# The second expert layer under a manual schedule, with whole 256-token units from the start and raw buffers given out by a planner

## The chip, the cores and the metric

The kernel runs on one core of one Trainium2 chip. The time is that of one execution on the device, in microseconds (us), from one launch; several executions are made and their median is given. Engines are named as in the profile: PE (matmul) and PEld (its weight loads), DVE, ACT, POOL, and SP, which only issues transfers here.

## What is computed

Three stages follow each other. The change touches the third.

```python
x = _attn_ref(q, k, v)                       # windowed attention with block sums, 2 x 8 x 768 x 64
x = x.transpose(0, 2, 1, 3).reshape(1536, 512)
x = _moe_ref(x, **moe)                       # each token through the one expert that its gate picks
# _moe2_ref: N = 1536 tokens, D = 512, E = 8 experts, F = 1024
logits = x @ w_gate
P = np.exp(logits - logits.max())
for _ in range(8):                           # rows, then columns, eight rounds
    P /= P.sum(1, keepdims=True) + 1e-09
    P /= P.sum(0, keepdims=True) + 1e-09
    P *= N / E
for e in range(E):                           # every token through every expert
    h = np.maximum(x @ w1[e], 0.0)
    out += P[:, e:e + 1] * (h @ w2[e])
```

## The kernel before

**Products.** Both products of an expert are done with seven block products in place of eight (sums and differences of operand blocks, Strassen's way), each operand as a high and a low f16 part, so three matmuls for each block. Tokens are taken in two halves of 768, each cut into three chunks of 256 columns. A unit is one chunk of one expert: its first products are 4 pieces (`fc`) of 7 block products of 6 matmuls, 168 matmuls in all, and its second products are 2 times 7 block products of 12 matmuls, again 168. `first(u, fc, i)` (line 1227 holds its matmul) and `second(e, k, s, i)` (line 1314) emit one block product each, and the ACT or DVE instruction that takes its result out of PSUM.

**Units before.** The first chunk of expert 0 is cut into two units of 128 columns, so that the first can begin when one block of 128 tokens is there: 25 units, `LEAD` = 1 more than 24.

**Ticks.** A list of ticks orders the emission: 28 a unit, one first product a tick. Other work is put on ticks by `at(tick, f)` and is emitted ahead of the product of that tick. Second products follow by a credit, in the long run one for two ticks. A product's block sums (lines 1247 to 1284) come 8 to 18 ticks after its piece began.

**PSUM.** The block products of a piece share two tiles (`x`, and `a` with its halves y and z), and results are taken out between the products that go into the same place: three ticks, or at the least two, lie between.

**Who decides the order.** An engine runs its instructions in the order of its own queue, and waits at the one whose inputs aren't there. Before, the whole block is emitted in ticks, and Tile's scheduler then sets each engine's order out of its own estimate of when each instruction is ready; the emission is only its priority. Around the blocks, one `issue_after` pins an instruction behind another.

**Weights.** For each expert 8 pieces (`Piece`) are brought in by SP (`load`, lines 677 to 683) into one of three buffers, `raws`, squared by ACT for a scale (`measure`, line 691; `rate`, line 697), negated by ACT (`signs`, line 707) and summed by accumulating transfers that POOL issues from SBUF to SBUF (`add`, line 702; `chain(1)` to `chain(3)`, each upon the result of the one ahead). ACT then writes the high parts (`hi`, line 724, as `raw_hi` and `sum_hi`) and DVE the low parts (`lo`, line 729). Offsets of these steps in ticks, and which of the three buffers a piece uses, are written out by hand (`lay`). The scaled result of a second product is written to one of two `y` tiles by ACT (line 1352) and added to `acc` by an accumulating transfer of POOL's (lines 1346, 1354).

**Tokens and routing.** `tokens(j)` brings one pair of 128-token blocks (`load`), turns them by PE (`turn`, line 1057, ACT copy 1064), makes the seven operands (`operands`: DVE 1077 to 1086, ACT casts 1069, low parts 1070 on POOL or DVE) and the `logits`. `mixing()` is the routing: 5 steps to start, 8 rounds of two, an end.

Of the kernel before, what the change touches and what calls it, by code (L numbers as in the profile page):

```python
# [108 lines left out]
def body(ctx: ExitStack, tc: tile.TileContext, q, k, v, wg1, w1a, w2a, wg2, w1b, w2b, cst, out):  # L109
# [928 lines left out]
    def tokens(j):  # L1038
# [3 lines left out]
        xw, ps, tmp = [], [], []  # L1042
# [10 lines left out]
        def turn():  # L1053
            for half in range(2):
                p = pg.tile([P, KC, P], F32, tag="x", name="pt")
                for kc in range(KC):
                    nc.tensor.transpose(p[:, kc], xw[half][:, kc * P : (kc + 1) * P], ident)
                t = half * HTB + j
                nc.gpsimd.tensor_copy(xinv[:, t : t + 1], xw[half][:, DM : DM + 1])
                if half == 0:  # L1060
                    tmp.append(raws[2].rearrange("p a f -> p (a f)"))
                to = tmp[0] if half == 0 else xw[0]
                to = to[:, :DM].rearrange("p (k t) -> p k t", k=KC)
                nc.scalar.copy(to, p)
                ps.append(to)
# [6 lines left out]
        def operands():  # L1072
            t4 = tmp[0][:, DM:].rearrange("p (k t) -> p k t", k=2 * KC)
# [125 lines left out]
    def spot(u, b):  # L1199

        seq = u - LEAD - CHUNKS + 1
        if seq < 0:
            return sets[UNITS[u][1]], b
        return (xh, xl), (7 * seq + b) % 8
# [7 lines left out]
    def first(u, fc, i):  # L1212

        e, k, o, n = UNITS[u]
# [9 lines left out]
        p = s["x"][:, :n] if place == "x" else s["a"][:, "zy".index(place), :n]  # L1224
        for kc in range(K2):
            for m, (l, r) in enumerate(((wh, sh), (wh, sl), (wl, sh))):
                nc.tensor.matmul(  # L1227
                    p, l[:, a, kc * P : (kc + 1) * P], r[:, j, kc, o : o + n], start=new and kc == 0 and m == 0,
                    stop=kc == K2 - 1 and m == 2, skip_group_check=True,
                )  # L1230
        c, k_ = s["c"][:, :, :n], kap[e % 2][:, fc : fc + 1]
# [13 lines left out]
        elif i == 4:  # L1245
            add(slice(C1, C0 + 1), s["a"][:, :, :n])
# [8 lines left out]
    def operands2(u, fc):  # L1255

        e, k, o, n = UNITS[u]
        c = st.pop((u, fc))["c"][:, :, :n]
# [3 lines left out]
        def raw_hi():  # L1262
            if o == 0:
                old = CHUNKS * e + k - 2
                while old >= 0 and rest and rest[0][:2] <= divmod(old, CHUNKS):
                    second(*rest.pop(0))
                hs[e, k, fc] = tuple(hg.tile([P, 7, CN], F16, tag=x, name="h" + x) for x in "hl")
            h.extend(x[:, :, o : o + n] for x in hs[e, k, fc])
# [104 lines left out]
    ra, rb, rc = raws  # L1373
    spare = [acc[:, t : t + 2].rearrange("p a (b d) -> p (a b) d", d=Q) for t in (4, 10)]
    for e in range(1, E):
        s = TICKS * (LEAD + CHUNKS * e)
        p1, p2, level = weights(e)

        def lay(p, raw, load, measure=True, begin=None):
            at(s + load, lambda: p.load(raw))  # L1380
            if measure:
                junk = raw[:, 4:6].rearrange("p a f -> p (a f)") if raw in raws else acc[:, 3]
                at(s + load + 5, lambda: p.measure(junk.bitcast(BF16)))
                at(s + load + 8, p.rate)
            if begin is None:
                return
            at(s + load + 6, p.signs)
            mid = load + 11
            if p.second:
                at(s + mid, lambda: p.chain(1))  # L1390
                mid += 4
            at(s + mid, lambda: p.chain(2))
            if p.second and p.j == F2 - 1:
                last[e] = p
                return
            begin = max(begin, load + 9)
            at(s + begin, p.raw_hi)
            at(s + begin + 1, p.raw_lo)
            end = max(mid + 4, begin + 3)
            at(s + end, lambda: p.chain(3))  # L1400
            at(s + end + 4, p.sum_hi)
            at(s + end + 5, p.sum_lo)

        if e == 1:
            lay(p2[0], rb, -45, begin=-30)
            lay(p2[1], ra, -40, begin=-30)
            lay(p1[0], rc, -32, begin=-15)
            lay(p2[3], spare[0], -22)
            lay(p1[3], spare[1], -22)
            lay(p1[1], rb, -19, begin=-8)  # L1410
            lay(p2[2], spare[0], -14)
            lay(p1[2], ra, -13, begin=-1)
            lay(p1[3], rc, -4, False, begin=6)
            lay(p2[2], rb, 2, False, begin=0)
            lay(p2[3], ra, 10, False, begin=0)
        else:
            lay(p2[3], rc, -66)
            lay(p2[0], rb, -58, begin=-45)
            lay(p2[1], rc, -52, begin=-45)
            lay(p2[2], ra, -45, begin=0 - 45)  # L1420
            lay(p1[0], rb, -32, begin=-15)
            lay(p1[3], rc, -26)
            lay(p1[1], rc, -19, begin=-8)
            lay(p1[2], ra, -13, begin=-1)
            lay(p1[3], rb, -4, False, begin=6)
            lay(p2[3], ra, 10, False, begin=0)
        at(s - 3, level)
        for k in range(CHUNKS):
            u = LEAD + CHUNKS * e + k
            b0 = TICKS * (u - 1)  # L1430
            for j, b in enumerate(ORDER):
                at(b0 + 5 if j == 0 else b0 + 7 * (F2 - 1) + FIRST[j - 1][0] + 1, lambda u=u, b=b: refill(u, b))

# [9 lines left out]
    COST2 = 3 * F2 * 109  # L1443
    LAG = 6 * 218 * 6
    ended = {}
    now = credit = 0
    for tick in range(max(ticks) + 8):
        for f in plan.pop(tick, ()):
            f()
        if tick in ticks:  # L1450
            u, fc, i = ticks[tick]
            e, k, o, n = UNITS[u]
            first(u, fc, i)
            cost = 6 * (109 if n == CN else 56)
            now += cost
            credit = min(credit + cost, COST2)
            if (fc, i) == (F2 - 1, 6):
                ended[e, k, o // P] = now
                if n == CN:
                    ended[e, k, 1] = now  # L1460
        if rest and (credit >= COST2 or rest[0][:2] == (0, 0)):
            e, k, s, i = rest[0]
            if now >= ended.get((e, k, s), now) + LAG:
                second(*rest.pop(0))
                credit -= COST2
                now += COST2
    for x in rest:
        second(*x)
    rest.clear()
# [24 lines left out]
```

## Time and profile before

| | us |
|---|---|
| median of 2 runs (lowest, highest) | 1427.23 (1426.74, 1427.72) |
| the profiled execution's own time | 1419.92 |
| its span, first to last instruction | 1418.1 |
| PE busy / PEld busy | 1237.8 / 1073.8 |
| DVE / ACT / POOL busy | 924.4 / 893.0 / 389.0 |
| mean granted clock of TensorE | 0.953 |

The busy times overlap. A matmul's record is longer than its place in the pipeline, so a PE that is busy in every row is not yet at its full pace. An idle row is put down to the engine that released it; idle time costs something only on the engine that sets the end.

### The profile page before, as it was taken

What the parts mean: (1) busy time and instruction counts of PE and PEld (TensorE: products, weight loads), DVE (VectorE), ACT (ScalarE), POOL (GpSimd) and SP (SyncE); (2) the same over time, 40 slices, a digit from 0 to 9 for tenths busy, and PEclk for the clock granted to TensorE, in tenths of its full rate; (3) what the DMA queues carried; (4) which work ended last, traced back from release to release, by engine and by line L of the source; (5) the groups of instructions that cost most, each with busy time, mean ns of one, the idle gap of its engine ahead of it and who ended that gap; (6) DMA issues with size and microseconds to landing.
All of it is one profiled execution on the core that took longest, in us unless ns stands there. A gap on an engine that the chain in (4) does not pass through costs nothing.

```text
span 1418.1 us, 28331 instructions
## 1 busy us (share of the span) xinstructions
PE 1237.8 (87%) x10719; PEld 1073.8 (76%) x10719; DVE 924.4 (65%) x1825; ACT 893.0 (63%) x1691; POOL 389.0 (27%) x450
## 2 busy tenths in 40 slices
PE   6898877898889897889888897988798889789998
PEld 5776776788777786778777776877686778678887
DVE  6775655565878876666666656667566656666665
ACT  5685656665768677666766666666667666656541
POOL 4443222312322222331423232233312331321000
PEclk8999998899999999999999999999999999999999
DMA  9946886764545656575766576566747565753311
GB/s 208 198 99 212 259 235 197 210 189 151 169 149 121 130 142 154 111 159 122 162 149 137 107 152 153 120 143 131 162 104 168 118 135 125 156 120 88 82 47 53
DMA packets 213040, 206.67 MB, mean 146 GB/s; under 512 B 36816, under 2 KB 184144, under 8 KB 212512
## 3 DMA queue, kind: packets, MB, share of 16 engines
q1 hardware_dynamic: 162464, 143.22, 34.9%
q0 software_dynamic: 50432, 61.56, 26.2%
q8 instruction: 86, 1.41, 0.4%
q14 instruction: 58, 0.48, 0.1%
HBM read 135.57 MB, written 15.53 MB: 107 GB/s over the span
## 4 chain that ended last, share of the span: by engine, by line
PE 28%; DMA 19%; issue 11%; DVE 8%; ACT 6%; POOL 2%; SPq 1%; POOLq 0%; ACTq 0%; DVEq 0%
DMA raw<-raw 12%; PE gx L1314 8%; PE fx L1227 8%; PE ga L1314 6%; PE fa L1227 5%; DMA raw<-in_moe_w 5%; DVE w1l L729 3%; POOL raw L702 2%; ACT w1h L724 2%; ACT raw L691 1%; ACT w2h L724 1%; DVE w2l L729 1%; DMA xh<-xohd 1%; ACT c L1234 1%; DMA xl<-xold 1%
## 5 line engine op out<-in xcount | busy, mean ns | idle before, releaser
L1227 PEld LDWEIGHTS <-w1h 128*128 128x128 f16 x2800 | 270.3, 99 | 149.7 <-issue 113.6
L702 POOL DMA_DIRECT2D raw<-raw x256 | 226.0, 978 | 539.7 <-DMA raw<-raw 206.1
L1314 PEld LDWEIGHTS <-hh 128*128 128x128 f16 x2688 | 269.1, 100 | 45.7 <-issue 9.0
L1227 PE MATMUL fx<-xh,w1h 128*128 128x256 f16 (+1 forms) x768 | 207.5, 273 | 91.8 <-ACT c L1234 90.4
L1314 PE MATMUL gx<-w2h,hh 128*128 128x256 f16 x768 | 213.4, 278 | 4.0 <-ACT y L1352 2.3
L1314 PE MATMUL gx<-w2l,hh 128*128 128x256 f16 x768 | 213.4, 278 | 0.0
L1314 PE MATMUL gx<-w2h,hl 128*128 128x256 f16 x768 | 213.1, 278 | 0.0
L1227 PE MATMUL fx<-xh,w1l 128*128 128x256 f16 (+1 forms) x768 | 208.3, 274 | 0.0
L1227 PE MATMUL fx<-xl,w1h 128*128 128x256 f16 (+1 forms) x768 | 208.1, 273 | 0.0
L1234 ACT ACTIVATE c<-fx,kap 128x256 f32<-128x256 f32 (+1 forms) x300 | 136.4, 460 | 55.5 <-PE fx L1227 52.3
L1227 PE MATMUL fa<-xh,w1h 128*128 128x256 f16 (+1 forms) x576 | 155.2, 272 | 12.1 <-ACT c L1234 9.2
L1314 PE MATMUL ga<-w2h,hh 128*128 128x256 f16 x576 | 161.6, 281 | 2.9 <-ACT acc L1338 2.6
L1284 DVE TENSOR_TENSOR hl<-c,hh 128x1024 f16<-128x1024 f32 (+1 forms) x100 | 118.1, 1181 | 70.3 <-ACT hh L1281 69.6
L1314 PE MATMUL ga<-w2l,hh 128*128 128x256 f16 x576 | 161.4, 280 | 0.0
L1314 PE MATMUL ga<-w2h,hl 128*128 128x256 f16 x576 | 161.2, 280 | 0.0
L1227 PE MATMUL fa<-xh,w1l 128*128 128x256 f16 (+1 forms) x576 | 154.7, 271 | 0.9 <-DVE w1l L729 0.9
L1227 PE MATMUL fa<-xl,w1h 128*128 128x256 f16 (+1 forms) x576 | 155.0, 271 | 0.0
L1227 PEld LDWEIGHTS <-w1l 128*128 128x128 f16 x1400 | 138.8, 99 | 18.2 <-DVE w1l L729 1.2
L1314 PEld LDWEIGHTS <-hl 128*128 128x128 f16 x1344 | 134.5, 100 | 18.4
L1281 ACT CAST hh<-c 128x1024 f16<-128x1024 f32 (+1 forms) x100 | 101.0, 1010 | 58.2 <-DVE c L1278 57.7
L1272 DVE SCALAR_TENSOR_TENSOR hl<-c,hh 128x768 f16<-128x768 f32 (+1 forms) x100 | 94.1, 941 | 55.2 <-ACT hh L1269 55.2
L724 ACT ACTIVATE w1h<-raw,wsc 128x768 f16<-128x768 f32 (+1 forms) x64 | 66.7, 1042 | 92.8 <-DMA raw<-raw 66.3
(249 smaller groups left out, 2550.7 us busy)
## 6 DMA issues: line engine op xcount, KB each, us to landing
raw<-in_moe_w SPq DMA_DIRECT2D x64, 512.0 KB, 4.3
raw<-raw POOLq DMA_DIRECT2D x256, 128.0 KB, 3.7
raw<-in_moe_w SPq DMA_DIRECT2D x228, 128.0 KB, 3.3
xh<-xohd SPq DMA_DIRECT2D x147, 128.0 KB, 3.4
xl<-xold SPq DMA_DIRECT2D x147, 128.0 KB, 3.2
acc<-y POOLq DMA_DIRECT2D x72, 256.0 KB, 4.0
raw<-in_moe_w SPq DMA_DIRECT2D x38, 256.0 KB, 3.8
vt<-in_v SPq DMA_DIRECT2D x16, 240.0 KB, 8.1
```

What stands on the lines that cost most here:

```text
L691: nc.scalar.activation(junk, raw, AF.Square, accum_out=ssq_)
L702: nc.gpsimd.dma_start(out=self.raw[:, to], in_=self.raw[:, of], accum_op=ALU.add)
L724: nc.scalar.activation(self.dst()[0][:, w], self.raw[:, s], AF.Copy, scale=wsc[self.x][:, self.i : self.i + 1])
L729: nc.vector.scalar_tensor_tensor(out=lo[:, w], in0=self.raw[:, s], scalar=wsc[self.x][:, self.i : self.i + 1], in1=hi[:, w], op0=ALU.mult, ...
L1227: nc.tensor.matmul(p, l[:, a, kc * P : (kc + 1) * P], r[:, j, kc, o : o + n], start=new and kc == 0 and m == 0, stop=kc == K2 - 1 and m == ...
L1234: nc.scalar.activation(c[:, q], p, f, scale=k_)
L1272: nc.vector.scalar_tensor_tensor(out=h[1][:, :3], in0=raw, scalar=0.0, in1=h[0][:, :3], op0=ALU.max, op1=ALU.subtract)
L1281: nc.scalar.copy(h[0][:, 3:], c)
L1284: nc.vector.tensor_tensor(out=h[1][:, 3:], in0=c, in1=h[0][:, 3:], op=ALU.subtract)
L1314: nc.tensor.matmul(p, l, r, start=new and f == 0 and m == 0, stop=f == F2 - 1 and m == 2, skip_group_check=True)
```

## The change

The third stage is emitted under `tc.manual_schedule()`: each engine's order is the order of emission, and no scheduler moves it. Expert 0 has three units of 256 columns as the others have, so two pairs of token blocks are loaded, turned and made into operands ahead of the first product (70 small matmuls on ones stand between their loads and their turns), with scratch tiles of their own for the second pair. The other four pairs and the routing get new ticks. The three raw buffers are given out by a planner: each piece has a tick at which it is wanted, and gets the buffer that is free first; `load` is put at that tick or when the buffer is free, and the other steps at fixed distances (square 5, rate 8, signs 6, chains 11 and 15, high parts 4 ticks behind the last chain).

```diff
-        xw, ps, tmp = [], [], []
+        xw, ps = [], []
+        if j == 1:
+            tmp = yp.tile([P, DM], F32, tag="y", name="x1"), tp.tile([P, 4, CN], F32, tag="c", name="x4").rearrange("p a f -> p (a f)")
+        else:
+            t_ = raws[2].rearrange("p a f -> p (a f)")
+            tmp = t_[:, :DM], t_[:, DM:]
...
-                p = pg.tile([P, KC, P], F32, tag="x", name="pt")
+                p = (pf_ if j == 1 else pg).tile([P, KC, P], F32, tag="x", name="pt")
...
-    UNITS = [(0, 0, 0, P), (0, 0, P, P)] + [(0, k, 0, CN) for k in range(1, CHUNKS)]
-    UNITS += [(e, k, 0, CN) for e in range(1, E) for k in range(CHUNKS)]
-    LEAD = len(UNITS) - E * CHUNKS
+    UNITS = [(e, k) for e in range(E) for k in range(CHUNKS)]
...
     pairs = [tokens(j) for j in range(HTB)]
     mix = mixing()
+    pairs[0][0]()
+    pairs[1][0]()
     warm(pz, "m", 70)
-    for f in pairs[0][:3]:
-        f()
-    pairs[1][0]()
-    for j, ticks in enumerate(((0,), (2, 4, 20), (8, 28, 30, 46), (32, 40, 42, 48), (44, 57, 61, 64), (61, 64, 66, 72))):
+    for i in (1, 2):
+        pairs[0][i]()
+        pairs[1][i]()
+    for j, ticks in enumerate(((2,), (4,), (0, 3, 6, 20), (1, 12, 15, 24), (20, 33, 36, 48), (21, 42, 45, 52))):
         for tick, f in zip(ticks, pairs[j][-len(ticks) :]):
             at(tick, f)
-    for i, f in enumerate(mix):
-        at(74 + 2 * i, f)
+    turns = [76 + t + 5 * i for i in range(8) for t in (-3, 0)]
+    for tick, f in zip([52, 54, 58, 62, 66] + turns + [115], mix):
+        at(tick, f)
...
-            at(s + load, lambda: p.load(raw))
-            if measure:
...
-            lay(p2[3], rc, -66)
-            lay(p2[0], rb, -58, begin=-45)
-            lay(p2[1], rc, -52, begin=-45)
...
+            jobs += [(s - 70, p2[3], None, True), (s - 58, p2[0], s - 45, True), (s - 52, p2[1], s - 45, True), (s - 45, p2[2], s - 45, True)]
+            jobs += [(s - 32, p1[0], s - 15, True), (s - 26, p1[3], None, True), (s - 19, p1[1], s - 8, True), (s - 13, p1[2], s - 1, True)]
+            jobs += [(s - 4, p1[3], s + 6, False), (s + 10, p2[3], -99, False)]
...
+    free = [47] * len(raws)
+    for want, p, begin, measure in sorted(jobs, key=lambda x: x[0]):
+        i = min(range(len(raws)), key=lambda i: (max(free[i], want), -free[i]))
+        load = max(free[i], want)
+        s = TICKS * CHUNKS * p.e
+        at(load, lambda p=p, i=i: p.load(raws[i]))
+        if measure:
+            junk = raws[i][:, 4:6].rearrange("p a f -> p (a f)").bitcast(BF16)
+            at(load + 5, lambda p=p, junk=junk: p.measure(junk))
+            at(load + 8, p.rate)
...
+        if begin is not None:
+            at(load + 6, p.signs)
+            mid = load + 11
+            if p.second:
+                at(mid, lambda p=p: p.chain(1))
+                mid += 4
+            at(mid, lambda p=p: p.chain(2))
...
+                begin = max(begin, load + 9)
+                at(begin, p.raw_hi)
+                at(begin + 1, p.raw_lo)
+                end = max(mid + 4, begin + 3)
+                at(end, lambda p=p: p.chain(3))
+                end += 5
+                at(end - 1, p.sum_hi)
+                at(end, p.sum_lo)
...
-    for tick in range(max(ticks) + 8):
-        for f in plan.pop(tick, ()):
-            f()
...
+    with tc.manual_schedule():
+        for tick in range(max(ticks) + 8):
+            for f in plan.pop(tick, ()):
+                f()
```

In the kernel after, expert e begins with tick 84 e.

## Rows read from the trace of the kernel before

**Rows 1.** Windows: length, busy (count) of PE, PEld, DVE, ACT, POOL; clock, DMA share, GB/s.
```profile
359.50:467.58 108.08, 96.96 (x1107) 84.56 (x1105) 90.55 (x234) 85.39 (x185) 33.86 (x36) 0.98 0.54 147
467.58:609.08 141.50, 123.33 (x1065) 105.73 (x1063) 99.77 (x220) 95.14 (x165) 42.04 (x48) 0.95 0.61 134
609.08:1314.02 704.94, 620.44 (x5419) 538.75 (x5416) 448.30 (x812) 455.67 (x781) 198.81 (x228) 0.96 0.63 135
1314.02:1387.47 73.45, 73.14 (x670) 65.24 (x668) 49.74 (x87) 37.62 (x60) 2.61 (x3) 1.00 0.20 58
1387.47:1418.10 30.63, 26.08 (x235) 22.66 (x232) 14.03 (x26) 3.22 (x4) 0.00 (x0) 1.00 0.14 52
```

**Rows 2.** Window of line 1227 (first products) alone, PE and PEld.
```profile
609.08:1314.02 704.94, 347.75 (x2689) 264.92 (x2688) 0.96 0.63 135
```

**Rows 3.** Waits of PE from 609.08 to 1314.02: total us, times, longest.
```profile
PE fx L1227 <- ACT c L1234: 74.1, 35, 5.0
PE fa L1227 <- ACT c L1234: 8.3, 8, 2.3
PE gx L1314 <- ACT y L1352: 2.0, 3, 0.9
```

**Rows 4.** Waits of ACT from 609.08 to 1314.02.
```profile
ACT w1h L724 <- DMA raw<-raw: 52.4, 19, 4.6
ACT hh L1281 <- DVE c L1278: 36.8, 42, 1.9
...
ACT raw L691 <- DMA raw<-in_moe_w: 27.2, 20, 4.0
ACT c L1247 <- DVE c L1237: 25.8, 32, 1.3
ACT w2h L724 <- DMA raw<-raw: 25.5, 7, 5.6
```

**Rows 5.** Timeline of ACT: start, us, instruction, idle before it and releaser.
```profile
714.34 0.47 ACT L1234 ACTIVATE c<-fx,kap 128x256 f32<-128x256 f32 x1 [0.33 <-PE fx L1227]
717.09 1.15 ACT L724 ACTIVATE w1h<-raw,wsc 128x1024 f16<-128x1024 f32 x1 [2.27 <-DMA raw<-raw]
```

**Rows 6.** Timeline of POOL in the same microseconds.
```profile
713.76 0.86 POOL L702 DMA_DIRECT2D raw<-raw  x1 [1.72 <-DVE w1l L729]
```

**Rows 7.** The page's transfers: count, KB of one, median us from issue to landing.
```profile
raw<-raw POOLq DMA_DIRECT2D x256, 128.0 KB, 3.7
raw<-in_moe_w SPq DMA_DIRECT2D x228, 128.0 KB, 3.3
...
acc<-y POOLq DMA_DIRECT2D x72, 256.0 KB, 4.0
```

**Rows 8.** Groups by form from 609.08 to 1314.02: busy us, mean ns, idle before.
```profile
L702 POOL DMA_DIRECT2D raw<-raw x164 | 144.5, 978 | 310.6 <-DMA raw<-raw 120.8 <-ACT raw L707 99.0 <-DVE w1l L729 35.2
...
L1234 ACT ACTIVATE c<-fx,kap 128x256 f32<-128x256 f32 x193 | 89.1, 466 | 31.4 <-PE fx L1227 29.6 <-PE pf L697 1.7
...
L1352 ACT ACTIVATE y<-gx,pws 128x256 f32<-128x256 f32 x128 | 59.6, 466 | 18.8 <-PE gx L1314 18.8
```

**Rows 9.** Timeline of PE: the third stage's first matmul on a low part.
```profile
361.04 0.22 PE L1227 MATMUL fx<-xl,w1h 128*128 128x128 f16 x1
```

**Rows 10.** Groups from 353 to 420, ACT's and POOL's work on token blocks.
```profile
L1070 POOL TENSOR_TENSOR xl<-raw,xh 128x512 f16<-128x512 f32 x7 | 9.7, 1444 | 8.4 <-ACT xh L1069 8.3
L1069 ACT CAST xh<-raw 128x512 f16<-128x512 f32 (+1 forms) x16 | 8.6, 565 | 1.5 <-DVE raw L1081 1.5
...
L1064 ACT COPY raw<-pt 128x512 f32<-128x512 f32 x12 | 7.0, 593 | 11.3 <-PE pt L1057 11.3
```

**Rows 11.** Timeline of ACT, a result of a unit of 128 columns.
```profile
362.18 0.36 ACT L1234 ACTIVATE c<-fx,kap 128x128 f32<-128x128 f32 x1
```

**Rows 12.** Windows of 20 us: one with a long wait of PE's, one without.
```profile
1220.00:1240.00 20.00, 15.02 (x115) 12.14 (x113) 10.43 (x21) 11.84 (x21) 6.41 (x9) 0.83 0.78 153
1300.00:1320.00 20.00, 20.00 (x185) 17.93 (x184) 11.21 (x19) 12.05 (x21) 1.72 (x2) 1.00 0.45 117
```

More of the change, by code (lines that the diff above doesn't have):

```diff
@@ L1262, in raw_hi @@
         def raw_hi():
[L1263 to L1268, printed above, removed]
+            while u >= 2 and rest and rest[0][:2] <= UNITS[u - 2]:
+                second(*rest.pop(0))
+            h.extend(hg.tile([P, 7, CN], F16, tag=x, name="h" + x) for x in "hl")
+            hs[e, k, fc] = h
             nc.scalar.activation(h[0][:, :3], raw, AF.Relu)
@@ L1369, in body @@
             at(tick, f)
-    for i, f in enumerate(mix):
-        at(74 + 2 * i, f)
+    turns = [76 + t + 5 * i for i in range(8) for t in (-3, 0)]
+    for tick, f in zip([52, 54, 58, 62, 66] + turns + [115], mix):
+        at(tick, f)
     last = {}
-    ra, rb, rc = raws
     spare = [acc[:, t : t + 2].rearrange("p a (b d) -> p (a b) d", d=Q) for t in (4, 10)]
+    jobs = []
     for e in range(1, E):
-        s = TICKS * (LEAD + CHUNKS * e)
+        s = TICKS * CHUNKS * e
         p1, p2, level = weights(e)
-        def lay(p, raw, load, measure=True, begin=None):
-            at(s + load, lambda: p.load(raw))
-            if measure:
[L1382 to L1402, printed above, removed]
-        if e == 1:
[L1405 to L1415, printed above, removed]
-        else:
-            lay(p2[3], rc, -66)
-            lay(p2[0], rb, -58, begin=-45)
-            lay(p2[1], rc, -52, begin=-45)
[L1420 to L1427, printed above, removed]
@@ L1428, in body @@
+        at(s - 2, level)
         for k in range(CHUNKS):
[L1429 removed]
+            u = CHUNKS * e + k
             b0 = TICKS * (u - 1)
@@ L1432, in body @@
                 at(b0 + 5 if j == 0 else b0 + 7 * (F2 - 1) + FIRST[j - 1][0] + 1, lambda u=u, b=b: refill(u, b))
+    free = [47] * len(raws)
[8 more added lines that the diff above has]
+            at(load + 8, p.rate)
+            assert load + 8 <= s - 3, (p.e, p.second, p.j, load - s)
+            end = load + 5
+        if begin is not None:
[5 more added lines that the diff above has]
+            at(mid, lambda p=p: p.chain(2))
+            if p.second and p.j == F2 - 1:
+                last[p.e] = p
+                end = s + 39
+                assert mid < s + 30, (p.e, p.second, p.j, mid - s)
+            else:
+                begin = max(begin, load + 9)
[6 more added lines that the diff above has]
+                at(end, p.sum_lo)
+                assert end <= s + (39 if p.second else 7 * p.j + 1), (p.e, p.second, p.j, end - s)
+                assert begin <= s + (37 if p.second else 7 * p.j - 1), (p.e, p.second, p.j, begin - s)
+        free[i] = end + 1
     ticks = {}
@@ L1442, in body @@
             rest += [(e, k, s, i) for s in range(2) for i in range(7)]
-    COST2 = 3 * F2 * 109
-    LAG = 6 * 218 * 6
+    COST1, COST2 = 3 * K2 * 109, 3 * F2 * 109
+    LAG = 6 * (COST1 + COST2 // 2)
     ended = {}
     now = credit = 0
-    for tick in range(max(ticks) + 8):
-        for f in plan.pop(tick, ()):
-            f()
[L1450 to L1469, printed above, removed]
+    with tc.manual_schedule():
+        for tick in range(max(ticks) + 8):
+            for f in plan.pop(tick, ()):
+                f()
+            if tick in ticks:
+                u, fc, i = ticks[tick]
+                e, k = UNITS[u]
+                first(u, fc, i)
+                now += COST1
+                credit = min(credit + COST1, COST2)
+                if (fc, i) == (F2 - 1, 6):
+                    ended[e, k] = now
+            if rest and (credit >= COST2 or rest[0][:2] == (0, 0)):
+                e, k, s, i = rest[0]
+                if now >= ended.get((e, k), now) + LAG:
+                    second(*rest.pop(0))
+                    credit -= COST2
+                    now += COST2
+        for x in rest:
+            second(*x)
+        rest.clear()
     assert not plan, sorted(plan)
```

31 lines of the change are left out of this document (17 added, 14 removed).

## The prediction

> **What bounds the kernel now.** I read the windows by stretch first. The third stage goes from 359.5 to 1418.1 us, and its cuts fall on the first products of an expert or a unit: expert 0 takes 108.08 us, expert 1 141.50, the next 16 units 704.94, the last two units 73.45, the tail of second products 30.63 [rows 1]. The 16 units are known by their 2689 first products, 168 to the unit [rows 2]. The reader should see two things. The last two units, where no weights are prepared any more, run 670 PE records in 73.45 us at clock 1.00: 0.1096 us for one, 36.7 us a unit. The 16 units ahead of them take 44.1 each, though they do the same products. At 0.1096 us their 5419 records would take 594 us, so 111 us of the 704.94 are lost; expert 1's 1065 records would take 117, so 25 are lost.
>
> Next come the waits. In the 16 units PE waits 84.4 us, nearly all for an ACT instruction that should have cleared PSUM [rows 3]. The mean clock is 0.96 there; with two levels, full and half, that is half clock for 8% of the stretch, 56 us, of which half is lost: 28 us. The sum of 84.4 and 28 is 112, so the loss is accounted for. Then ACT's own waits: 105.1 us for transfers of weights, up to 5.6 us at a time (52.4, 25.5 and 27.2 us), and 62.6 for DVE, none over 1.9 us [rows 4]. ACT is busy 455.67 of 704.94 us and DVE 448.30 [rows 1], so neither is full. ACT stops at a weight piece, its queue holds the clearing of PSUM behind it, and PE runs dry.
>
> One case shows how. POOL issued the last accumulating transfer of a piece at 713.76 [rows 6]; ACT's writing of the sums' high part was next on its queue, waited 2.27 us and began at 717.09 [rows 5], that is 3.3 us after the issue. The emission puts the two four ticks apart; a tick at full pace is 36.7 / 28 = 1.31 us, so 5.2 us. The scheduler had moved them together: the order which ran is not that of the emission, and it counts on transfers quicker than the chip's 3.3 to 3.7 us [rows 7].
>
> **The parts, with their costs.** The sum is made against the profiled execution's own 1419.92 us; the median of the runs is 7.3 above it, and that is added at the end. Attention and the first expert layer aren't touched: 0.
>
> *The 16 units.* The manual order removes no instruction and adds none; it puts each at its tick. Squares stand 5 ticks behind their load (6.5 us; four issues and a landing of 3.3 [rows 7]), a chain's link 4 ticks or more behind the one ahead and the high part 4 behind the last link: 5.2 us against 3.7 to landing [rows 7], which leaves 1.5 us for POOL's own queue, where one issue takes 0.98 [rows 8]. Two issues ahead of it would use that up, so a rest of waits stays. On the other side, a product of the same PSUM place comes two or three ticks later, some 2.6 us, and an ACT result takes 0.47 [rows 8], so a wait of about 2 us on ACT is free. The order between loads, refills and the other buffers' loads on SP stays that of ticks, and SP has little to do. Bounds: 111 us gained if nothing is left; nothing gained if ACT's waits only change places. I take 85%, since what goes is the waits over 2 us and what stays is the rest of 1 us or less: -94. The clock's 28 us go with the waits in this, since it stood at 1.00 in a stretch of unbroken products and at 0.83 around a wait of 5 us [rows 12].
>
> Here the Trainium skill gives another measure. Rows first: PE's matmul records cover 620.44 of the 704.94 us, weight loads 538.75, or 76.4%, against 65.24 of 73.45, or 88.8%, at full pace [rows 1]. The page "Perfetto Trace Analysis", section "Identifying the Most-Contended Engine", says that matmul busy time judges headroom badly, as matmuls are pipelined, and that weight-load busy time is the better measure. By matmul records 84.5 us are open, by the page 704.94 x (1 - 76.4 / 88.8) = 98, by the count of products 111; at 85% that would be 72, 84 and 94. The trace bears the page out against the matmul records, and the count goes a step further.
>
> The skill also has a price for the chain's transfers. "DMA: Bandwidth & Descriptors", section "Anatomy of one DMA — SWDGE (gpsimd) path", fits 2.0 us plus the bytes over 436e3; for 128 KB that is 2.3 us, an estimate by that page. The row has 3.7. By the page the four ticks leave 2.9 us and no rest of waits, and the 16 units would give the whole 111; the sum goes by the row.
>
> *Expert 1.* The same mechanism with the end of the routing beside it: 25 us lost, at 85% -21, bounds 0 and -25. Its first pieces come at other ticks than later ones; ACT's 95.14 us and DVE's 99.77 in 141.50 [rows 1] still fit into 120.
>
> *The start.* Before, the first product came at 359.5 [rows 1] with half the columns, and its low-part matmuls only at 361.04 [rows 9], when POOL's difference was there. After, it needs the second pair as well. Behind the first pair ACT does two copies (0.59 each) and four more casts (0.57) ahead of that [rows 10], 3.4 us, then POOL's difference of 1.44 as before. DVE's sums lie between the casts: up to 2.5 more. PE then stands still for about 5 us between turning the tokens and its first product, and such a gap was followed by a clock of 0.83 over 20 us, 3.4 us lost [rows 12]. Together +3.4 to +9.3; I take +6.
>
> *Expert 0.* Two units of 128 columns become one of 256: the same columns for PE, 168 matmuls fewer, nothing gained there. For ACT a result of 128 columns takes 0.36 us [rows 11] and one of 256 takes 0.47 [rows 8], so a pair costs 0.25 more than one; at 16 such results in the unit, and some 12 longer instructions of each engine with the like saving, 5 to 7 us of ACT and as many of DVE go away. DVE is the fullest engine here, 90.55 of 108.08 us [rows 1], with tokens' and routing work on it. The tokens' transfers on SP wait for the raw buffers, as before; they can start ahead of their tick, as SP waits for nothing else. Moving this work earlier by ticks puts more on the first unit, where no second product stretches the ticks: ACT and DVE will bind it. Bounds: PE's idle 11.1 us gained, or, at the density that DVE reaches in expert 1 (99.77 of 141.50, 71%), 90.55 / 0.71 = 128, 20 lost. I take -5.
>
> *The planner.* It only moves some loads by a few ticks; each piece's steps keep their distances, and the weights' last part is still written ahead of its first use by 6 ticks or more. 0, with the two bounds inside those of the 16 units. *Last units and tail*: same work, 0.
>
> Sum: -94 - 21 + 6 - 5 = -114. 1419.92 - 114 = 1306, plus 7.3: **1313 us**.
>
> **Rivals.** (a) *ACT and DVE in lockstep.* With fixed orders ACT's 62.6 us of waits for DVE [rows 4] can't be filled with other work any more and pass to PE in full: 16 units take 594 + 63 = 657, a gain of 48, expert 1 gains 10, the start as above: 1419.92 - 57 + 7.3 = 1370. For it: ACT would be busy 455.67 of 594, 77%, and no stretch of before runs unbroken at that density. Against it: those waits are under 1.9 us each, and the PSUM distance covers 2.
>
> (b) *The change doesn't do what it says.* If the order that ran is in the main the emission's, only latencies count and nothing moves: 1427, between 1400 and 1450. For it: the distances in ticks are those of before. Against it: the case of 713.76 to 717.09 [rows 5, 6].
>
> (c) *Slower: POOL's queue in strict order.* A chain's link that waits for the one ahead now holds the accumulation of `y` into `acc` behind it; a `y` tile comes back late, ACT waits ahead of line 1352 and holds PE. There are 72 such transfers [rows 7]. If each came 2.5 us late, that is 180 us, and 1427 - 114 + 180 = 1493. It decides from 114 / 72 = 1.6 us each. For it: POOL waited 120.8 us for its own chains in 164 issues [rows 8]. Against it: PE waited only 2.0 us on `y` before [rows 3], and a tile has about 6 ticks, 7.9 us, against an issue and 4.0 to landing [rows 7].
>
> **How the numbers follow.** Forecast 0.70, (a) 0.13, (b) 0.10, (c) 0.07. The forecast's lower end: the 16 units and expert 1 lose nothing more (-136), expert 0 gains 11, the start costs 3: 1419.92 - 144 + 7 = 1283; and the fullest 20 us hold 185 records at 0.108 [rows 12], against 0.1096, which takes another 8 from the 16 units: 1275. The upper end takes in (a), 1370, with the 20 us that expert 0 could lose: 1390. So 1275 to 1390, which leaves out (b) and (c). A measurement of this kernel tells 2% from no change. Faster by over 2%, below 1399: the forecast, (a) and a little of (b), 0.83. Slower by over 2%: 0.07. Between: 0.10.
>
> **What would show it.** Right: a unit of experts 2 to 6 near 38 us; PE's waits on line 1234 under 20 us in those units, ACT's waits for weight transfers under 25, clock 0.99, weight loads busy 86% or more. The first product of the stage around 364 to 367; expert 0 about 108 us from its first product. Wrong would be: ACT's waits for transfers as before (then the order wasn't the cause), or gone while PE still waits for line 1234, now behind DVE (a), or POOL's line 702 with ACT's line 1352 behind it (c), or an expert 0 of 120 us and more, with DVE full. What could upset the forecast most is the density of ACT and DVE, which no stretch of before shows at full pace.

## The result, and the profile after

The changed kernel takes 1362.89 us (median of 2 runs, 1360.79 and 1365.00) against 1427.23: 0.9549 of before, interval 0.9484 to 0.9614. The forecast was 1313, its range 1275 to 1390. The gain is 64 us where 114 were expected. The profiled execution's own time is 1360.79, so the sum to account for is 1419.92 - 1360.79 = 59.1.

The windows of the kernel after, cut as those of before [rows 1] (length, then busy and count of PE, PEld, DVE, ACT, POOL, then clock, DMA share, GB/s). Lines 1 to 3 are the units of expert 0, 4 to 6 those of expert 1, then the 16 units, the last two, the tail:

```profile
365.80:401.70 35.90, 28.35 (x281) 23.59 (x281) 25.64 (x46) 20.78 (x41) 8.88 (x12) 0.80 0.44 163
401.70:449.00 47.30, 41.83 (x392) 36.34 (x390) 32.49 (x65) 29.61 (x59) 8.98 (x10) 0.93 0.29 86
449.00:492.10 43.10, 34.05 (x280) 28.07 (x279) 33.26 (x94) 30.23 (x54) 10.58 (x13) 0.92 0.63 149
492.10:538.80 46.70, 42.55 (x375) 36.86 (x373) 40.12 (x94) 27.02 (x48) 12.25 (x15) 0.96 0.55 119
538.80:581.20 42.40, 38.93 (x343) 33.91 (x341) 31.58 (x62) 32.27 (x56) 11.20 (x13) 0.96 0.56 125
581.20:624.50 43.30, 38.39 (x342) 33.64 (x340) 28.86 (x60) 30.58 (x53) 15.27 (x18) 0.96 0.76 161
624.50:1246.10 621.60, 597.89 (x5418) 528.19 (x5417) 456.54 (x818) 450.60 (x787) 203.34 (x233) 1.00 0.71 155
1246.10:1319.40 73.30, 72.12 (x661) 64.49 (x660) 50.34 (x87) 35.91 (x60) 2.61 (x3) 1.00 0.22 62
1319.40:1359.00 39.60, 29.05 (x243) 24.35 (x240) 15.01 (x27) 3.31 (x4) 0.00 (x0) 0.91 0.11 41
```

Against [rows 1] the stage splits like this (us):

| | forecast | measured | before to after |
|---|---|---|---|
| start | +6 | +6.3 | first product at 359.5, 365.8 |
| expert 0 | -5 | +18.2 | 108.1, 126.3 |
| expert 1 | -21 | -9.1 | 141.5, 132.4 |
| 16 units | -94 | -83.3 | 704.9, 621.6 |
| last two units | 0 | -0.1 | 73.4, 73.3 |
| tail | 0 | +9.0 | 30.6, 39.6 |
| sum | -114 | -59.0 | |

So the 16 units did nearly what was forecast, and 44 of the missing 55 us lie outside of them. The waits of PE in the 16 units (total, times, longest), to set against 74.1 and 8.3 us in [rows 3]:

```profile
PE fx L1227 <- ACT c L1234: 13.1, 18, 1.4
PE pf L697 <- DVE sqb L692: 9.6, 11, 1.5
PE fa L1227 <- ACT c L1234: 0.3, 1, 0.3
```

The waits of ACT there, to set against [rows 4]:

```profile
ACT hh L1279 <- DVE c L1276: 28.8, 23, 3.7
ACT w1h L724 <- DMA raw<-raw: 27.5, 16, 3.7
...
ACT raw L691 <- DMA raw<-in_moe_w: 23.6, 16, 2.8
ACT w2h L724 <- DMA raw<-raw: 15.0, 5, 3.3
```

ACT still waits 27.5 + 23.6 + 15.0 = 66.1 us for transfers (105.1 before), but PE's wait for the clearing of PSUM is down from 82.4 to 13.4 and the clock is 1.00. By the page both kinds of transfers land later than before; the chain's was 3.7 and the load's 3.3 [rows 7]. A second profile of the same kernel has 3.9 for the chain, so this difference alone isn't the reason for ACT's waits; it is looked for below:

```profile
raw<-raw POOLq DMA_DIRECT2D x256, 128.0 KB, 4.5
raw<-in_moe_w SPq DMA_DIRECT2D x228, 128.0 KB, 3.8
```

By the Trainium skill's page "Perfetto Trace Analysis", section "Identifying the Most-Contended Engine", weight-load busy time is the better measure of what is open: 528.19 / 621.60 = 85.0% here against 64.49 / 73.30 = 88.0% in the last two units. By that, an estimate of 21 us is left in the 16 units; a later run found 25 (18.6 against the second profile), so the traces agree with the page.

In expert 0 PE's waits from 365.8 to 492.1 name few places:

```profile
PE fa L1227 <- ACT c L1234: 9.5, 2, 5.1
PE pf L697 <- DVE gsc L627: 4.9, 2, 2.7
PE fx L1227 <- ACT xh L1071: 3.4, 1, 3.4
```

ACT's timeline at the first of them (start, length, instruction, idle before it):

```profile
384.76 0.61 ACT L1071 CAST acc<-raw 128x512 f16<-128x512 f32 x1
388.62 1.49 ACT L1071 CAST acc<-raw 128x512 f16<-128x512 f32 x3 [3.26 <-DVE raw L1080]
390.01 0.40 ACT L1087 CAST bh<-raw 128x256 f16<-128x256 f32 x1
390.32 0.63 ACT L1247 ACTIVATE c<-c 128x512 f32<-128x512 f32 x1
390.85 0.45 ACT L1234 ACTIVATE c<-fa,kap 128x256 f32<-128x256 f32 x1
```

A token pair's casts (`acc` and `bh` in the lines) stand as one block on ACT's queue, because they are emitted on one tick. ACT stops 3.26 us inside the block until DVE has the operands ready, and the clearing of `fa`, for which PE waits, stands behind the block. The cause is that of before, with another owner: then a weight piece held the queue, now a token pair does.

The tail, on DVE's timeline and PE's:

```profile
1326.80 1.23 DVE L1282 TENSOR_TENSOR hl<-c,hh 128x1024 f16<-128x1024 f32 x1 [1.11 <-ACT hh L1279]
1327.94 0.48 DVE L1342 SCALAR_TENSOR_TENSOR acc<-ga,pws,acc 128x256 f32<-128x256 f32 x1
...
1328.47 0.37 PE L1312 MATMUL ga<-w2h,hh 128*128 128x256 f16 x1 [4.86 <-DVE acc L1342]
```

The closing ticks hold the sums of the last piece and no second product, as the credit grows with first products alone. So DVE's queue has all those sums ahead of the result that frees PE's place: 4.86 us of stand, and then half clock (mean 0.91 in the tail).

### The profile page after: what moved, and what is told of

Same layout as the page of the kernel before. It is cut to its first block, busy times and chain, and to the rows that moved or that the text cites. A ratio compares the mean times of both kernels' runs of the same rounds, so it can differ in the third digit from the quotient of the medians.

```text
span 1359.0 us, 27981 instructions
## 1 busy us (share of the span) xinstructions
PE 1220.4 (90%) x10551; PEld 1066.1 (78%) x10551; DVE 938.3 (69%) x1793; ACT 879.6 (65%) x1663; POOL 388.7 (29%) x450
## 4 chain that ended last, share of the span: by engine, by line
PE 23%; DMA 15%; issue 8%; ACT 7%; DVE 4%; SPq 1%; POOL 1%; ACTq 0%; POOLq 0%; DVEq 0%
DMA raw<-raw 9%; PE gx L1312 7%; PE fx L1227 6%; PE ga L1312 5%; DMA raw<-in_moe_w 5%; PE fa L1227 4%; ACT hh L1279 2%; ACT raw L691 2%; ACT c L1234 1%; DMA acc<-y 1%; POOL raw L702 1%; DVE acc L1342 1%; DVE w2l L729 1%; ACT raw L707 1%; DVE w1l L729 1%
## 5 line engine op out<-in xcount | busy, mean ns | idle before, releaser
L1312 PEld LDWEIGHTS <-hh 128*128 128x128 f16 x2688 | 264.8, 99 | 47.4 <-issue 15.2
L1227 PE MATMUL fx<-xh,w1h 128*128 128x256 f16 x736 | 202.7, 275 | 21.7 <-ACT c L1234 16.7
L1227 PE MATMUL fx<-xl,w1h 128*128 128x256 f16 x736 | 202.9, 276 | 1.4 <-POOL xl L1072 1.4
L1227 PE MATMUL fx<-xh,w1l 128*128 128x256 f16 x736 | 202.8, 276 | 0.0
L1234 ACT ACTIVATE c<-fx,kap 128x256 f32<-128x256 f32 x288 | 132.2, 470 | 58.0 <-PE fx L1227 52.6
L1227 PE MATMUL fa<-xh,w1h 128*128 128x256 f16 x552 | 152.5, 276 | 4.7 <-ACT c L1234 4.7
L1227 PE MATMUL fa<-xl,w1h 128*128 128x256 f16 x552 | 152.6, 276 | 0.0
L1227 PE MATMUL fa<-xh,w1l 128*128 128x256 f16 x552 | 152.4, 276 | 0.0
L1282 DVE TENSOR_TENSOR hl<-c,hh 128x1024 f16<-128x1024 f32 x96 | 117.3, 1222 | 49.0 <-ACT hh L1279 48.9
L1312 PEld LDWEIGHTS <-hl 128*128 128x128 f16 x1344 | 132.4, 99 | 16.2
L1279 ACT CAST hh<-c 128x1024 f16<-128x1024 f32 x96 | 99.8, 1040 | 43.7 <-DVE c L1276 43.3
L790 DVE TENSOR_TENSOR wl<-raw,wh 128x1024 fp32r<-128x1024 f32 x64 | 78.1, 1223 | 41.3 <-ACT wh L789 38.4
```

Source lines behind the costliest of these rows:

```text
L790: nc.vector.tensor_tensor(out=lo, in0=raw, in1=hi.bitcast(F32), op=ALU.subtract)
L1227: nc.tensor.matmul(p, l[:, a, kc * P : (kc + 1) * P], r[:, j, kc], start=new and kc == 0 and m == 0, stop=kc == K2 - 1 and m == 2, skip_gr ...
L1234: nc.scalar.activation(c[:, q], p, f, scale=k_)
L1279: nc.scalar.copy(h[0][:, 3:], c)
L1282: nc.vector.tensor_tensor(out=h[1][:, 3:], in0=c, in1=h[0][:, 3:], op=ALU.subtract)
L1312: nc.tensor.matmul(p, l, r, start=new and f == 0 and m == 0, stop=f == F2 - 1 and m == 2, skip_group_check=True)
```

## The experiments

Each run stands beside runs of the kernel before on the same chip (medians 1427.6 to 1432.5). Its stages are cut as above (`e0`, `e1`: experts 0 and 1); whatever the run, the last two units take 73.3 or 73.4.

| run | first product | e0 | e1 | 16 units | tail | median | ratio, interval |
|---|---|---|---|---|---|---|---|
| e1_before_manual | 367.5 | 155.2 | 118.0 | 623.7 | 39.5 | 1380.57 | 0.9648 (0.9591, 0.9704) |
| e2_after_auto | 371.3 | 110.9 | 139.2 | 720.9 | 30.5 | 1443.05 | 1.0084 (1.0058, 1.0111) |
| e3_tail | 367.5 | 124.4 | 133.4 | 612.4 | 33.2 | 1345.47 | 0.9408 (0.9359, 0.9456) |
| e4_spread | 365.7 | 119.4 | 131.8 | 615.9 | 39.3 | 1346.72 | 0.9421 (0.9370, 0.9472) |
| e5_late | 366.5 | 125.9 | 132.1 | 596.5 | 39.7 | 1336.67 | 0.9368 (0.9324, 0.9412) |
| e6_no_rounds | 370.0 | 121.3 | 126.1 | 616.0 | 39.9 | 1347.63 | 0.9432 (0.9390, 0.9475) |
| e8_fine_tail | 367.0 | 122.1 | 132.2 | 614.7 | 33.1 | 1343.81 | 0.9416 (0.9379, 0.9453) |
| e9_after_again | 367.1 | 125.7 | 132.4 | 615.1 | 39.3 | 1356.30 | 0.9500 (0.9465, 0.9534) |
| e10_warm | 365.7 | 126.2 | 128.2 | 624.4 | 40.1 | 1362.49 | 0.9544 (0.9503, 0.9584) |
| e11_all | 370.2 | 119.3 | 132.3 | 596.7 | 32.7 | 1323.94 | 0.9259 (0.9224, 0.9293) |
| e12_all_warm | 367.5 | 120.8 | 131.4 | 597.7 | 32.7 | 1320.96 | 0.9249 (0.9218, 0.9281) |
| e13_mixed | 369.0 | 110.1 | 136.1 | 595.0 | 32.8 | 1315.59 | 0.9192 (0.9160, 0.9224) |

**Which part gives the gain.** e1_before_manual is the kernel before with its own hand-made ticks under the fixed order, and nothing else:

```
+    with tc.manual_schedule():
         for tick in range(max(ticks) + 8):
```

> The kernel before with one thing changed: its expert block is emitted under the manual schedule; ticks, half units and hand-given raw buffers stay. Theory M, the fixed order itself gives the gain: the 16 units of experts 2 to 6 and the first of 7 take 39 us each (620 to 640 in all, 704.9 before, 621.6 after), PE's waits on line 1234 there fall from 82 us to under 25, and the whole is 1350 to 1385, depending on what expert 0 loses. Rival P, the planner and the new ticks give it: the units stay at 43 us or more and the whole at 1410 or more.

e2_after_auto is the changed kernel with the order left to the scheduler:

```
-    with tc.manual_schedule():
+    if True:
```

> The kernel after with one thing undone: the block is left to the scheduler again; planner, ticks and whole units stay. Theory M: the 16 units go back to 43 to 45 us each, ACT waits again some 100 us for weight transfers in them, the whole is 1410 to 1435. Rival P: units near 39 us, the whole at 1380 or less.

The window of the 16 units of e2_after_auto, then the waits of PE and of ACT in it:

```profile
621.30:1342.20 720.90, 624.06 (x5419) 540.42 (x5417) 447.51 (x812) 454.19 (x781) 198.60 (x228) 0.96 0.61 132
```

```profile
PE fx L1227 <- ACT c L1234: 87.8, 41, 5.6
```

```profile
ACT w1h L724 <- DMA raw<-raw: 45.4, 18, 5.2
ACT w2h L724 <- DMA raw<-raw: 37.7, 7, 7.8
...
ACT raw L691 <- DMA raw<-in_moe_w: 30.4, 23, 2.9
```

The fixed order by itself brings the units of before from 44.1 to 39.0 us; without it the changed kernel has 45.1 and the waits of before. It is a little slower than before, and than expected, so planner, whole units and spread work bring nothing without the order. Under the order they are worth 18 us (the medians of e1_before_manual and of the changed kernel): experts 0 and 1 together take 273.2 us on the old ticks and 258.7 on the new. The split between the two experts can't be compared: on the old ticks in fixed order 77 of the routing's 86 DVE instructions run ahead of expert 1, on the new ticks 36. What else is to be seen is expert 0 under the scheduler, 110.9 against 126.3, and the tail, 30.5 against 39.6: there the fixed order loses.

**The tail.** e3_tail lets second products come out in the closing ticks too:

```
-            if rest and (credit >= COST2 or rest[0][:2] == (0, 0)):
+            if rest and (credit >= COST2 or rest[0][:2] == (0, 0) or tick > max(ticks)):
```

> The kernel after, but in the ticks behind the last first product a second product is emitted in every tick; in the kernel after these ticks hold the last piece's sums alone, and all second products left come behind them. Theory T, in the fixed order the clearing of PSUM stands on DVE's queue behind those sums, which wait for ACT in turn: the stretch from the last first product to the end falls from 39.6 us to 31 to 33, PE's wait of 4.9 us there goes, and the whole loses 6 to 9 us. Rival: more second products are left over at the end than before, and the stretch stays over 38.

The tail of e3_tail:

```profile
1310.90:1344.20 33.30, 27.07 (x244) 23.57 (x241) 14.65 (x27) 3.31 (x4) 0.00 (x0) 0.97 0.13 48
```

It goes from 39.6 to 33.2 and the wait of 4.86 us is gone; what remains over 30.6 is 2.6. The rest of the gain in the median (0.9408 against 0.9549) is in the 16 units, which came out at 612 to 624 us in all kernels that have the same order there: the changed kernel again, e9_after_again, had 615.1.

> The kernel after, once more, beside these on one chip: 1360 to 1365 us by what was measured; its 16 units show how much they vary from run to run (621.6 in one profile, 612 to 616 in kernels with the same orders there).

**Expert 0.** e4_spread cuts the operands of a token pair into three steps with ticks of their own:

```
+        def operands1():
...
             parts((B11, B21), c1, nc.gpsimd)
...
+        def operands2_():
...
             parts((T1, T2), t4[:, : 2 * K2], nc.vector)
             parts((B22,), b22, nc.vector)
+
+        def operands3():
...
             parts((T3, T4), t4[:, 2 * K2 :], nc.gpsimd if j else nc.vector)
             nc.scalar.copy(bh, b12)
...
-    for j, ticks in enumerate(((2,), (4,), (0, 3, 6, 20), (1, 12, 15, 24), (20, 33, 36, 48), (21, 42, 45, 52))):
+    for j, ticks in enumerate(((2,), (4,), (0, 3, 6, 8, 10, 20), (1, 12, 15, 17, 19, 24), (20, 33, 36, 38, 40, 48), (21, 41, 43, 45, 46, 52))):
```

> The kernel after, but a token pair's operands are emitted as three steps, for pairs 2 to 5 on ticks of their own one to two apart, in place of one lump. Theory L, the lump holds ACT and DVE so long that PE waits for its PSUM: expert 0, first product to first product of expert 1, falls from 126.3 us to 112 to 118, and the waits of 4.4 and 5.1 us on line 1234 there go; the whole loses 8 to 14 us. Rival R, the routing's rounds on DVE and the single small PSUM bank are what costs: expert 0 stays at 122 or more. Rival W, the whole first unit: its 35.9 us stay, the rest too.

Expert 0 falls from 126.3 to 119.4, a little short of what was expected: the lump is a cause, for about 6 us (the repetition had 125.7). The waits of 4.4 and 5.1 us, which were to go, are still 3.2 each. e8_fine_tail makes six steps of a pair (each cast apart from its low part) and has the mended tail.

> The kernel after with the end mended as in the run before (a second product in every closing tick) and a token pair's operands in six steps, each ACT cast on a tick of its own and DVE's part of it a tick later; ahead of the first product the two pairs' steps take turns. Theory L: expert 0 falls to 110 to 115 us (126.3 in the kernel after, 119.4 with three steps), its first product comes 1 to 2 us earlier, the whole is 1328 to 1338. Rival R: three steps already gave what there was, expert 0 stays at 118 or more and the whole at 1340 or more.

With 122.1 it is no better than three steps, so the stronger form of that theory, that finer steps gain more, falls. e6_no_rounds leaves out the eight rounds of the routing (its weights are not balanced):

```
-        return [gates1, gates2, start1, start2, start3] + [turn1, turn2] * 8 + [end]
+        return [gates1, gates2, start1, start2, start3] + [end]
...
-    turns = [76 + t + 5 * i for i in range(8) for t in (-3, 0)]
+    turns = []
```

> The kernel after without the eight rounds of the routing (64 DVE instructions of some 0.2 us, 8 small matmuls): the output is that of unbalanced weights. Theory R, these rounds, in strict order on the fullest engine and through the one small PSUM bank, are what expert 0's last unit and expert 1's first lose: the two fall from 43 and 47 us to 39 and 41 or less, 8 us or more together. Rival L, the tokens' lumps and the weights of expert 1 are the cause: the two lose under 4 us together.

The two units that hold the rounds (the last of expert 0, the first of expert 1) go from 89.7 to 80.9, and both experts together lose 11.3 us; the first two units of expert 0 change little, 34.0 and 47.0 against 35.9 and 47.3. In the trace the rounds are 72 DVE instructions, some 16 us of DVE's time (not 64 instructions, as expected), and the run takes away this work along with its places in the order, so it doesn't price the places alone. e10_warm puts 34 small matmuls in the gap ahead of the stage's first product, against the half clock there:

```
+    warm(pz, "m", 34)
```

> The kernel after with 34 small matmuls on ones more, between the turning of the first two token pairs and the first product, where PE stands still for 3.6 us. Theory C, that gap drops the clock to half, and the first unit pays for it: the granted clock stays at 1.00 from 363 to 373 us (0.5 in the kernel after), the first unit falls from 35.5 us to 29 to 32, the whole loses 3 to 6 us. Rival: the unit is bound by ACT and DVE at its short ticks, the clock is there but the unit stays at 34 or more.

The first unit takes 35.9 us as before it. The stretch from 363.1 to 373.3, at half clock in the kernel after, is hardly better here; the kernel after, then e10_warm:

```profile
363.10:373.30 10.20, 6.12 (x50) 4.82 (x50) 7.57 (x12) 5.64 (x13) 4.59 (x5) 0.50 0.29 85
```

```profile
365.70:373.50 7.80, 6.74 (x53) 5.34 (x53) 5.15 (x9) 3.41 (x8) 2.81 (x4) 0.56 0.44 117
```

The clock stood at 1.00 up to the first product (360 to 365.7). But PE still waited 1.46 us ahead of that product and 1.04 behind it, and from 367.03 on its records are 0.37 to 0.42 us long, as at half clock in the kernel after, in place of 0.27. So the run shortened the gap without taking away the half clock, and what the clock costs the first unit stays open.

**The 16 units.** e5_late delays steps of the weights of experts 3 to 7. The square comes one tick later behind the load, and `signs` and all chain links move along with it, so the links keep their distance of 4 ticks; `rate` and `raw_hi` come two ticks later, and the high part of the sums 5 ticks behind the last link in place of 4:

```
+        late = int(p.e > 2)
...
-            at(load + 5, lambda p=p, junk=junk: p.measure(junk))
-            at(load + 8, p.rate)
+            at(load + 5 + late, lambda p=p, junk=junk: p.measure(junk))
+            at(load + 8 + 2 * late, p.rate)
...
+            at(load + 6 + late, p.signs)
+            mid = load + 11 + late
...
-                end += 5
+                end += 5 + late
```

> The kernel after, with later ticks for the weight pieces of experts 3 to 7: square one tick later, rate two, signs, chains one, high part of the sums one more behind the last chain. Theory D, what the 16 units still lose (39 us each against 36.7) is ACT and PE waiting for weight transfers that need 4.5 us and for the rate behind them: units of experts 3 to 6 fall to 37.3 to 38, PE's 9.6 us for line 697 and ACT's 66 us for transfers go down by half or more, the whole loses 8 to 14 us. Rival A, ACT and DVE in lockstep at their density: units stay at 38.4 or more, the whole within 4 us of the kernel after.

Window, PE's waits and ACT's waits for transfers in e5_late:

```profile
624.50:1221.00 596.50, 589.77 (x5418) 527.12 (x5416) 455.58 (x818) 452.61 (x787) 202.40 (x233) 1.00 0.74 162
```

```profile
PE fx L1227 <- ACT c L1234: 5.9, 10, 0.8
```

```profile
ACT w1h L724 <- DMA raw<-raw: 14.6, 11, 2.3
...
ACT raw L691 <- DMA raw<-in_moe_w: 7.0, 5, 2.1
```

The 16 units take 596.5 us, 37.3 each, beside 594 for the bare count of products. ACT is 452.61 / 596.50 = 76% busy and PE hardly held: rival (a) of the prediction has lost its ground. Which of the longer distances did it, no run separates.

**Together.** e11_all has the mends of e3_tail, e4_spread and e5_late; e12_all_warm adds the 34 small matmuls.

> The three mends together: later steps for the weights of experts 3 to 7, a second product in every closing tick, a token pair's operands in three steps. If each part's gain is its own and they add (19 for the units, 6 for the end, 6 for expert 0), the whole is 1322 to 1328 us. Rival: the gains share the same waits, and the whole stays at 1333 or more.

> As the run before, with the 34 small matmuls of the first run of this call. Theory C: 3 to 6 us under the run before it. Rival: within 2 us of it.

The gains add up; the small matmuls make no difference that can be told in the medians (3 us apart, their intervals overlap). In the first 7.8 us from the first product the clock is 0.78 with them and 0.56 without, and the first unit takes 31.1 us against 32.3. The last run leaves expert 0 to the scheduler and fixes the order from expert 1 on:

```
+    for part in (range(84), range(84, max(ticks) + 8)):
+        with tc.manual_schedule() if part.start else ExitStack():
+            for tick in part:
...
```

> This is the kernel of the three mends with the ticks of expert 0 left to the scheduler and the fixed order from expert 1 on. Theory S (a fixed order costs expert 0 because its short ticks are not laid out to the chip's waits; the scheduler's order took 110.9 us there): expert 0 falls from 119 to 108-113 us, the units stay at 37.3, and the whole comes out 6-11 us under the run of the three mends (1324): 1313-1318. Rival: the border between the two orders, or expert 0's own work (routing, transposes, whole pieces), costs as much as the fixed order does: expert 0 at 118 or more, the whole at 1322 or more.

The units of expert 0 and the whole of expert 1 in e13_mixed:

```profile
369.00:396.20 27.20, 25.79 (x266) 22.06 (x266) 23.29 (x45) 19.89 (x41) 9.79 (x12) 0.87 0.55 191
396.20:442.10 45.90, 41.58 (x393) 36.02 (x391) 32.41 (x70) 32.58 (x63) 15.71 (x15) 0.93 0.45 118
442.10:479.10 37.00, 31.23 (x279) 26.50 (x277) 26.44 (x78) 26.68 (x48) 4.77 (x6) 1.00 0.53 136
479.10:615.20 136.10, 123.22 (x1054) 106.12 (x1053) 101.31 (x218) 90.08 (x159) 39.77 (x46) 0.94 0.60 130
```

Expert 0 takes 110.1 (119.3 under the fixed order), its first unit 27.2 against 32.3. Expert 1 gives 3.8 back. At 0.9192 of before it is the fastest version, 1 - 0.9192 / 0.9549 = 3.7% below the changed kernel. Its interval and that of e11_all touch at 0.9224, and it overlaps that of e12_all_warm; the stages, not the wholes, separate them.

## Why the prediction came out as it did

**What bounds the kernel, and the 16 units: right.** The loss came from the scheduler's order (e1 and e2 show it from both sides), it went through ACT's queue into PE, and the clock came back with the waits. -94 was forecast, -83.3 measured (-89.8 in the second look, e9_after_again). The mis-sized part is "5.2 us against 3.7 to landing [rows 7], which leaves 1.5 us for POOL's own queue": ACT's waits for transfers stayed at 66.1 us, not under 25. A slower landing alone doesn't explain it: the page's median was 4.5 in this profile and 3.9 in that of e9_after_again, the same kernel, where ACT still waited 61.0. The forecast counted POOL's issues at 0.98 us and no wait of POOL's ahead of them. The longest of ACT's waits for a link, on POOL's timeline and ACT's:

```profile
1224.11 0.86 POOL L1352 DMA_DIRECT2D acc<-y  x1 [4.81 <-ACT y L1350]
1224.69 1.17 POOL L702 DMA_DIRECT2D raw<-raw  x1
```

```profile
1229.77 1.15 ACT L724 ACTIVATE w1h<-raw,wsc 128x1024 f16<-128x1024 f32 x1 [3.70 <-DMA raw<-raw]
```

POOL stood at the accumulation of a `y` tile, and the last link of the chain came behind it on its queue. So ACT reached the high part 1229.77 - 3.70 - 1224.69 = 1.4 us after the link's issue, where the ticks had laid four, 5.2 us, between. The same sequence stands once in each of experts 2 to 7 and makes 17.0 of the 27.5 us that ACT waits there for `w1h`. In e9_after_again, whose trace has the landings, the link ahead had landed 0.7 to 2.4 us before these issues, so a part of it is POOL's queue and the rest the links' own landings; no run took the one away from the other. The longer distances of e5_late brought ACT's waits for transfers to 14.6 + 7.0 = 21.6 us and the units to 37.3. The low bound, "nothing left", was within reach of the ticks.

The Trainium skill's fit ("DMA: Bandwidth & Descriptors", section "Anatomy of one DMA — SWDGE (gpsimd) path") would give an estimate of 2.3 us for these transfers; the medians of the traces are 3.4 to 4.9, so the measurement decides, and the distances in ticks have to be made from it.

**Expert 0: the step that was mis-sized.** "I take -5"; it was +18.2, near the upper bound of +20, which stood for a DVE as dense as in expert 1 (71%). The forecast counted what the instructions cost and asked whether DVE fills up. DVE didn't: it was busy 25.64 + 32.49 + 33.26 = 91.39 of 126.3 us, 72%, with 90.55 of work before [rows 1]. What the step left out is that the fixed order, which gains in the even units, loses where the ticks aren't laid out for the chip's waits: 126.3 with it, 110.9 and 110.1 without (e2, e13). Of those 16 us, 6 to 7 come from the token pairs' lump (e4). The other 9 are the order again, 5.1 in the first unit and 4.1 in the third (e11 against e13); e13 shows them as a whole, not wait by wait, and expert 1 gives 3.8 of them back.

**Expert 1: half of the forecast.** -21 was taken by "the same mechanism with the end of the routing beside it", and -9.1 came. More of the routing fell into this expert, 50 of its 86 DVE instructions against 37 before. Its rounds, work and places together, cost about 6 us here (126.1 without them); on the old ticks in fixed order, with 77 of the 86 already done, expert 1 took 118.0 (e1), near the 117 of the bare count. The two experts together went from 249.6 to 258.7. Some of the rest shows as waits at `rate`; DVE's timeline and PE's around one, beside the start of expert 2:

```profile
599.75 0.16 DVE L692 CAST sqb<-ssq 128x1 bf16<-128x1 f32 x1
603.76 0.16 DVE L692 CAST sqb<-ssq 128x1 bf16<-128x1 f32 x1 [3.85 <-ACT raw L691]
...
605.94 0.15 DVE L627 TENSOR_SCALAR gsc<-pf 128x1 int32<-128x1 int32 x1
...
606.14 0.16 PE L697 MATMUL pf<-sqb,ones_b 128*128 128x1 bf16 x1 [3.82 <-DVE gsc L627]
```

DVE stops for the next piece's square, the scale of the piece before is queued behind it, and PE's second `rate` waits for the one small PSUM place. This is read from the timeline; no run took it away.

**The start: right, in part by luck.** 365.8, inside 364 to 367, and PE's first waits are those named, for the second pair's casts (3.4 us on line 1071) and POOL's difference (1.4). But 2.4 of the +6.3 us come from ahead of the third stage, where nothing was changed: the last product of the first expert layer ends at 344.9 before and 347.3 after (345.9 to 352.3 in the other runs); PE's timeline of before, then of after:

```profile
344.54 0.39 PE L842 MATMUL py<-wh,hl 128*128 128x512 f32 x1
```

```profile
346.94 0.39 PE L842 MATMUL py<-wh,hl 128*128 128x512 f32 x1
```

From there to the first product it is 14.6 and 18.5 us, +3.9, at the low end of "+3.4 to +9.3". The clock's share in it, "3.4 us lost", stays open: half clock came, from 363.1 to 373.3, and no run took it away whole; where it was shorter, in e12_all_warm, the first unit was 1.2 us shorter.

**The tail: a step that failed.** "Last units and tail: same work, 0." The last units did, the tail lost 9.0. The work is the same, but the scheduler had moved second products between the last sums, and the emission doesn't. e3 gets 6.4 back.

**The rivals.** (a) gives 1370, close to the time, by the wrong mechanism: it wanted the loss in the 16 units (657; they took 621.6 and then 596.5) and none in the tail. (b), that the order doesn't change, falls with e1 and e2. (c), POOL's queue, falls as it was put: among PE's waits in the 16 units `y` isn't found. The trace has the reverse, `y` ahead of a chain's link (above). The sum missed by 55 us: 23 in expert 0, 12 in expert 1, 11 in the 16 units, 9 in the tail. That the time is inside the range is in part luck: its upper end, 1390, is rival (a)'s 1370 with expert 0's 20 us on top, while the forecast with expert 0 at that bound would be 1313 + 25 = 1338.

## What to carry to other kernels

A fixed order pays in the stretch that repeats, if each step stands behind the one that it waits for by the measured time, with a tick to spare. Measure that time in the kernel as changed, from the tick to the landing, with the waits that stand ahead of the issue on its own queue. In stretches that don't repeat (start, one-off work, tail) it turns every lump on one tick into a stop of the whole queue, so price these apart, and leave them to the scheduler, or spread them, if they come out longer. "Same work" is no reason for a cost of 0 when the order changes.

## What the runs showed of the hardware

The median landing time of the same 256 accumulating transfers of 128 KB was 3.4 us (e2_after_auto) to 4.9 (e1_before_manual): 3.7 before, 4.5 after, 3.7 in e5_late, 4.0 in e13_mixed. But the changed kernel had 4.5 in one profile and 3.9 in the other (e9_after_again), with a DMA share of 0.71 and 0.72 in the 16 units, so a difference of 0.6 between two kernels shows nothing. What sets the landing time stays open.

A DVE instruction was slow beside one of POOL's; DVE's timeline of the kernel after, then POOL's:

```profile
368.97 0.41 DVE L1072 TENSOR_TENSOR xl<-raw,xh 128x256 f16<-128x256 f32 x1
369.31 1.38 DVE L1088 TENSOR_TENSOR bl<-raw,bh 128x256 f16<-128x256 f32 x1
```

```profile
369.18 1.22 POOL L1072 TENSOR_TENSOR xl<-x,xh 128x512 f16<-128x512 f32 x1 [1.68 <-ACT xh L1071]
```

The same shape and operation takes 0.41 us and then 1.38, while POOL runs its own two-operand difference until 369.18 + 1.22 = 370.40. In e5_late the six instructions of line 1088 took 0.41 us twice, with none of POOL's differences beside them, and 1.21 to 1.37 four times, each beside one. The Trainium skill's page "SBUF — State Buffer", section "SBUF: two separate sides", says that a DVE instruction with two SBUF inputs and one of POOL's that reads SBUF exclude each other for a whole instruction. By that DVE would take 370.40 - 369.31 + 0.41 = 1.50 us, an estimate, against the 1.38 of the row, so the trace agrees; no run took POOL's work away to test it.

Under the fixed order, stages repeat closely where little waits for a transfer: the second unit of expert 0, where ACT waits 2.9 us for transfers, took 47.3 us in the kernel after and 47.4 in its repetition and in e5_late. The 16 units with the tight ticks differ by 12 us between kernels that have the same order there (612.4 to 624.4), with the distances of e5_late by 2.7 (595.0 to 597.7).
